# Attention, feed-forward and top-1 experts on one core: low-row folds one block later, the flags in three pieces, the second expert's first weights asked for ahead of its token rows

## The chip, the cores and the metric

The kernel runs on 1 core of one Trainium2 chip, as one launch. The metric is the device time of the launch in microseconds. Three timed runs of the kernel before took 589.20, 590.11 and 590.27 us; their median is 590.11 us. The engines are PE (matrix multiply), DVE (vector), ACT (scalar), POOL and SP; here SP only issues transfers, and POOL does some vector work and the indexed transfers.

## The reference

Three layers are chained. The last one, in which the change lies, is a top-1 mixture of experts over 1536 tokens of width 512, with 8 experts and a hidden width of 1024:

```python
q, k, v  # 2 batches, 8 heads, 768 tokens, head width 64
x = local_and_global_attention(q, k, v)      # 1536 x 512
x = (h * sigmoid(h)) @ w_out,  h = x @ w_in  # hidden width 2048
e_idx = argmax(x @ w_gate)                   # one expert for each token
for e in range(8):
    mask = e_idx == e
    h = np.maximum(x[mask] @ w1[e], 0.0)     # 512 -> 1024
    ye = h @ w2[e]                           # 1024 -> 512
    out[mask] = gate_w[mask, None] * eom[mask, e, None] * ye
```

Operands of matrix multiplies are split into a high and a low part (a rounded copy and the rest), and a product is the sum of high by high, high by low and low by high.

## The kernel before, in words

**Order of the experts.** `order` counts the tokens of each expert and sorts the experts by size. Place 0 is the largest; the places have windows of 320, 272, 248, 224, 208, 192, 184 and 176 rows. In what follows an expert is named by its place p, 0 to 7, so "the second expert" is place 1 and the last is place 7. The token rows, with their factor and their target row, stand sorted by expert in a DRAM buffer `xe`, written there by indexed transfers on POOL.

**One expert.** An expert is 8 blocks of 128 hidden columns, written (p,f) with f from 0 to 7. In the loop of `moe2`, `f1_mm` does the first multiply of a block into a PSUM bank `h` (L678 and L679 when the window is narrow, L684 otherwise); `f1_ev` takes it out: ACT copies the second half (`hs`, L690), DVE adds it (L691), ACT applies the relu and rounds (`hh` or, in the last expert, `hl`, L693), DVE makes the low part (L696). Two blocks later `f2_mm` uses the result in the second multiply into the banks `y` (L706 to L713). The PSUM banks of `h`, of the row turns `xm` and of the fold `yf` are taken in turn from the same four.

**Weights.** The 4 MB of an expert come as 16 units of 128x512, named 0 to 15. `load_u` asks for a unit on SP's queue into one of 8 buffers `qr` (L543); `split_u` has ACT make the high part (L548) and DVE, or POOL for every fourth unit, the low part (L549), which frees the buffer. The units of expert p+1 are split in the blocks f=2 to 7 of expert p (3, 3, 3, 3, 2 and 2 units). The units of an expert are asked for while the expert before it runs: 4 in block f=0, up to 8 in block f=1, and then as buffers come free.

**Rows.** `load_x(p)` asks on SP's queue for the token rows of an expert in tiles of 128 (L653; 3 tiles for the second expert), `load_t(0)` for factors and targets of the first expert (L657). Both read `xe`, so they wait for the last indexed transfer into it. `prep_x` turns the tiles with PE (`xm`, L668) in the blocks f=4 to 6, and ACT and DVE write high and low parts (`xwT`, L670, L671).

**The fold of the low rows.** For five places (0, 1, 5, 6, 7) the last 64 rows share one multiply: high rows give the lower half of a bank, low rows the upper half. `f2_ev` takes them out at the end of an expert: ACT writes `yl` (L721) and `y` (L723), and a function `fold` is put into the list `late`: PE moves the upper half down (`yf`, L727), DVE adds it (L728), POOL scatters the result to `out` (L635). `folds()` runs the list right behind the first multiply of a block. The list is filled in block f=1 of the next expert, so the fold is run in its block f=2; that of the last expert is run in the tail.

**Flags.** `flags` is 14 small DVE instructions (L508 to L521) that compute whether counts fit the windows; the result is read after the last expert (L1133), to decide on a slower general path. It is called in block (7,1), ahead of `f1_ev`.

Each engine takes its instructions in the order of the program, so an instruction that waits holds back all behind it on that engine.

Of the kernel before, what the change touches and what calls it, by code (L numbers as in the profile page):

```python
# [17 lines left out]
ALU = mybir.AluOpType  # L18
AX = mybir.AxisListType
# [4 lines left out]
def kernel(ctx, tc, qk, v, n_global, n_local, w_in, w_out, wg, w1, w2, out):  # L24
# [23 lines left out]
    NE,FF=w1.shape[0],w1.shape[2]  # L48
# [22 lines left out]
    flag=const.tile([P,10],I32,name="flag"); limk=const.tile([P,8],F32,name="limk"); pi=const.tile([P,4],I32,name="pi"); pf=const.tile([P,4],F32,name="pf")  # L71
    ordi=const.tile([P,8],I32,name="ordi"); first=const.tile([P,1],F32,name="first"); firstb=const.tile([P,1],F32,name="firstb"); cntf=const.tile([P,32],F32,name="cntf"); capk=const.tile([P,8],F32,name="capk")
    V=nc.vector; A=nc.scalar; G=nc.gpsimd; T=nc.tensor; S=nc.sync
# [411 lines left out]
    def order(c):  # L485
# [16 lines left out]
        if c==0:  # L502
            V.tensor_copy(first,i)
            V.tensor_scalar(out=first,in0=first,scalar1=-1.0,scalar2=8.0,op0=ALU.mult,op1=ALU.add)
    def flags():

        w=cntf[:,16:32]
        V.tensor_tensor(out=w[:,0:8],in0=w[:,0:8],in1=capk,op=ALU.subtract)  # L508
        V.tensor_scalar(out=s_flag[:,2:10],in0=w[:,0:8],scalar1=0.0,scalar2=None,op0=ALU.is_gt)
        V.tensor_tensor(out=w[:,0:8],in0=w[:,0:8],in1=limk,op=ALU.subtract)  # L510
        V.tensor_scalar(out=w[:,8:9],in0=pf[:,0:1],scalar1=-32.0,scalar2=None,op0=ALU.add)
        V.tensor_scalar(out=w[:,9:10],in0=pf[:,0:1],scalar1=-1.0,scalar2=None,op0=ALU.mult)
        V.tensor_scalar(out=w[:,10:11],in0=pf[:,2:3],scalar1=-97.0,scalar2=None,op0=ALU.add)
        V.tensor_scalar(out=w[:,11:12],in0=pf[:,2:3],scalar1=-1.0,scalar2=1.0,op0=ALU.mult,op1=ALU.add)
        V.tensor_tensor(out=w[:,12:16],in0=pf,in1=pf,op=ALU.mult)
        V.memset(w[:,12:13],0.0)
        V.memset(w[:,14:15],0.0)
        V.tensor_reduce(out=s_flag[:,1:2],in_=w,axis=AX.X,op=ALU.max)
        V.tensor_scalar(out=s_flag[:,1:2],in0=s_flag[:,1:2],scalar1=0.0,scalar2=None,op0=ALU.is_gt)
        V.tensor_reduce(out=s_flag[:,0:1],in_=s_flag[:,1:10],axis=AX.X,op=ALU.max)  # L520
        V.tensor_copy(flag,s_flag)  # L521
    s_flag=const.tile([P,10],F32,name="s_flag")


# [4 lines left out]
    def moe2_open2():  # L529
        es_m.close()  # L530
        m2['b']=es_2.enter_context(tc.tile_pool(name="m2b",bufs=1,side="left"))
    def ereg(p):
        if p not in reg: reg[p]=nc.values_load(ordi[0:1,p:p+1],engines=[mybir.EngineType.SP],min_val=0,max_val=NE-1)
        return reg[p]
    def wtile(name):
        return wp.tile([P,2,512],F32R,tag="wi",name=name,bufs=NWI)
    def load_u(k,i):

        p,q=divmod(k,4); hf=q//2; e=ereg(p)
        r=m2['a'].tile([P,512],F32,tag="qr",name="qr",bufs=NQR); uqr[k,i]=r  # L540
        if q%2==0: src=w1[ds(e,1),i*P:(i+1)*P,hf*512:(hf+1)*512].rearrange("o p f -> p (o f)")
        else: src=w2[ds(e,1),hf*512+i*P:hf*512+(i+1)*P,:].rearrange("o p d -> p (o d)")
        S.dma_start(r,src)  # L543
# [40 lines left out]
    def late_split():  # L584
        xr=xrp[NTT//2-1]
        for t in range(2): ea['l',t]=halves(xr[:,t,:512],(G,V)[t])
# [21 lines left out]
    def early1(hf,part):  # L608
        if part==0: ea['t']=s1bank([P,512],"eh")
        t=ea['t']; x=ea['xT']  # L610
        for k in range(6*part,6*part+6):
            ww,xx=((0,0),(0,1),(1,0))[k//4]; kc=k%4
            T.matmul(t,x[:,xx,kc,:],uq[2*hf,kc][:,ww],start=(k==0),stop=(k==11))
        if part==0: return
        h=m2['a'].tile([P,512],F32,tag="eh",name="ehs",bufs=2); ea['h',hf]=h
        A.activation(out=h,in_=t,func=AF.Relu)
# [13 lines left out]
    def early4():  # L630
        y=m2['a'].tile([P,512],F32,tag="eh",name="eyo",bufs=2)
        A.activation(out=y,in_=ea['y'],func=AF.Copy,scale=ea['x'][:,512:513])
        put(y,ea['x'][:,TOK:TOK+1].bitcast(I32),P)
# [4 lines left out]
    def tiles(p):  # L638

        a,z=R0[p],WIN[p]-(HALF if p in SMALL else 0)  # L640
        t=[(s,min(P,z-s)) for s in range(a,z,P)]+([(z,HALF)] if p in SMALL else [])
        return [(k,s,n) for k,(s,n) in enumerate(t)]
    def folded(p,k): return p in SMALL and k==len(tiles(p))-1
    xwt={}; xwT={}; ixt={}; sct={}
    def paired(p): return WIN[p]-R0[p]<PAIR
    def small(p):
        ixt[p]=m2['b'].tile([P,3],I32,tag="ix",name="ixt",bufs=4)
        sct[p]=m2['b'].tile([P,3],F32,tag="sc",name="sc",bufs=4)
    def load_x(p):
# [35 lines left out]
    def f1_ev(p,f,between=lambda: None):  # L685

        W=WIN[p]-R0[p]; t=h1.pop((p,f)); hh[p,f]=g=wtile("hl").rearrange("p a b -> p (a b)") if p==NE-1 else m2['b'].tile([P,2*WIN[1]],F32R,tag="hh",name="hh",bufs=HB)
        if paired(p):
            u=m2['b'].tile([P,WIN[1]],F32,tag="hs",name="hs",bufs=2)
            A.activation(out=u[:,:W],in_=t[:,W:2*W],func=AF.Copy)  # L690
            V.tensor_tensor(out=t[:,:W],in0=t[:,:W],in1=u[:,:W],op=ALU.add)  # L691
            between()
        A.activation(out=g[:,:W],in_=t[:,:W],func=AF.Relu)  # L693
        z=W-HALF if p in SMALL else W
        for a,b,o in ((0,z,2*W-z),(z,W,W)):
            if a<b: V.scalar_tensor_tensor(out=g[:,o:o+b-a],in0=t[:,a:b],scalar=0.0,in1=g[:,a:b],op0=ALU.max,op1=ALU.subtract)  # L696
        if not paired(p): between()
# [33 lines left out]
    def folds():  # L731
        while late: late.pop(0)()
    nq=[0,0]; NQR=8; NQB=4
# [11 lines left out]
    def moe2():  # L745
        late_split()
        early1(0,0)
        run_gates(2)
        early1(0,1)
        logits(NTT-2)  # L750
        early1(1,0)
        run_gates(1)
        late1()
        run_gates(1)
        early1(1,1)
        run_gates(1)
        early2(0)
        late3()
        order(1)
        moe2_open2()  # L760
        load_x(1); load_t(0)
        early3(0,0)
        early2(1)
        early3(0,1); early3(1,0)
        early3(1,1)
        early4()
        atags[0]=['s1','s1b','a','pv']
        LG=2
        steps=[(p,f) for p in range(NE) for f in range(8)]
        for g in range(len(steps)+LG):  # L770
            if g<len(steps):
                p,f=steps[g]
                def spl():
                    split_u(4*(p+1)+nq[1]//4,nq[1]%4,nq[1]%4==1); nq[1]+=1
                f1_mm(p,f)
                folds()
                if p+1<NE and f==0: nq[:]=[0,0]
                if g==len(steps)-7: flags()
                ns=(0,0,3,3,3,3,2,2)[f] if p+1<NE else 0
                f1_ev(p,f,spl if ns else lambda: None)  # L780
                if p+1<NE:
                    for _ in range(ns-1): spl()
                    while nq[0]<min(16,nq[1]+4*(f+1),nq[1]+NQR): load_u(4*(p+1)+nq[0]//4,nq[0]%4); nq[0]+=1
                    if p and f==0: load_x(p+1)
                    if p==0 and f==5:
                        for k,s,n in tiles(0): tail(0,k,xwt[0][:,k,0:1],xwt[0][:,k,1:2])
                    t=tiles(p+1)
                    px=PX
                    if px<=f<px+len(t): prep_x(p+1,t[f-px][0])
            if g>=LG:  # L790
                p2,f2=steps[g-LG]
                if p2<NE-1:
                    f2_mm(p2,f2)
                    if f2==7: f2_ev(p2)
                    continue
                big,last=tiles(p2)
                if f2==7: f2_mm(p2,0,[big])
                f2_mm(p2,f2,[last])
                if f2==7:
                    f2_ev(p2,[last])  # L800
                    for k in range(1,8):
                        f2_mm(p2,k,[big])
                        if k==2: folds()
                    f2_ev(p2,[big])
# [233 lines left out]
    with tc.manual_schedule():  # L1038
# [22 lines left out]
        steps=[(c,f) for c in range(len(CH)) for f in range(FB)]  # L1061
# [4 lines left out]
        def run_gates(k):  # L1066
            for _ in range(min(k,len(gq))): gq.pop(0)()
        for g in range(len(steps)+LAG):
            live=g<len(steps)
            if live:  # L1070
                c,f=steps[g]
# [110 lines left out]
```

## Time and profile before

| what | value |
|---|---|
| median of three timed runs | 590.11 us (589.20 to 590.27) |
| the profiled execution's own time | 588.92 us |
| its span, first to last instruction | 587.2 us |
| PE busy | 565.8 us (96%), 3939 matrix multiplies |
| DVE, ACT, POOL busy | 389.9, 302.9, 173.3 us |
| mean granted clock of PE | 0.992 of full speed |
| DMA | 106.74 MB, 182 GB/s over the span |

The busy shares are means over the whole span. The experts take its last third: the first multiply of the first expert starts at 395.12 us, the last at 569.41 us. Matrix multiplies overlap in the pipeline, so a busy PE is not a PE at its peak; what counts here is where PE sat idle and what ended the idle time. A row of a timeline gives the start and the length in us, the engine, the line, what is written and read, the count, and in brackets the idle time of that engine before it with what ended it.

### The profile page before, as it was taken

How to read it: one execution, taken by the hardware profiler on the slowest of the kernel's cores; microseconds unless marked ns; L12 is line 12 of the kernel's file. 1: busy time of each engine (PE TensorE's matmuls, PEld its weight loads, DVE VectorE, ACT ScalarE, POOL GpSimd, SP SyncE). 2: the span in 40 equal slices, each digit the busy share in tenths (PEclk: the TensorE clock that was granted, in tenths of full speed). 3: DMA queues.
4: the chain of work that ended last, by engine and by line, in shares of the span. 5: the costliest groups of instructions: out<-in, count | busy, mean ns of one | idle time of the engine just before them, and what ended most of it. 6: DMA issues, size and time to landing. Idle time of an engine off the chain costs nothing.

```text
span 587.2 us, 11814 instructions
## 1 busy us (share of the span) xinstructions
PE 565.8 (96%) x3939; PEld 475.4 (81%) x3939; DVE 389.9 (66%) x1088; ACT 302.9 (52%) x809; POOL 173.3 (30%) x214
## 2 busy tenths in 40 slices
PE   8999999999999999999999999999999999999983
PEld 3567888888888888888899999887787888887862
DVE  6885799998365756674645247646664887987940
ACT  7796334343444446343622326626656667767631
POOL 2367344443132431223111010213231332433311
PEclk9999999999999999999999999999999999999988
DMA  6666467697447877774473349219674668658400
GB/s 215 228 209 198 183 183 232 219 300 257 162 122 161 198 151 163 147 194 129 109 164 125 90 122 354 102 48 333 218 225 144 207 206 282 230 201 284 133 20 22
DMA packets 87530, 106.74 MB, mean 182 GB/s; under 512 B 35980, under 2 KB 50316, under 8 KB 87460
## 3 DMA queue, kind: packets, MB, share of 16 engines
q1 hardware_dynamic: 84692, 98.98, 56.8%
q0 software_dynamic: 2192, 6.39, 3.1%
q8 instruction: 33, 0.54, 0.4%
q10 hardware_dynamic: 576, 0.52, 0.3%
q14 instruction: 37, 0.30, 0.2%
HBM read 87.14 MB, written 17.66 MB: 178 GB/s over the span
## 4 chain that ended last, share of the span: by engine, by line
PE 64%; issue 10%; DVE 9%; ACT 6%; DMA 6%; POOL 3%; SPq 1%; POOLq 0%; DVEq 0%; ACTq 0%
PE s L339 19%; PE s L359 6%; PE s L360 6%; PE s L361 6%; PE qkp L170 3%; PE h L678 3%; DMA qr<-in_w_dram 3%; PE y L711 2%; PE y L713 2%; PE y L712 2%; PE pv L245 2%; PE h L684 2%; PE tp L206 2%; ACT uq L548 2%; PE h L679 2%
## 5 line engine op out<-in xcount | busy, mean ns | idle before, releaser
L339 PEld LDWEIGHTS s<-xT,wi 128*128 128x128 f32 x1152 | 147.4, 190 | 12.0 <-DVE g L348 5.6
L339 PE MATMUL s<-xT,wi 128*128 128x256 f32 x1152 | 152.0, 284 | 1.3 <-DVE xn L233 0.9
L343 ACT ACTIVATE u<-s 128x256 f32<-128x256 f32 x96 | 35.5, 381 | 102.6 <-PE s L339 100.8
L344 DVE SCALAR_TENSOR_TENSOR s<-u,s 128x256 f32<-128x256 f32 x96 | 39.7, 426 | 72.4 <-ACT u L343 72.4
L549 DVE TENSOR_TENSOR uq<-qr,uq 128x512 fp32r<-128x512 f32 x87 | 76.8, 902 | 8.0 <-ACT uq L548 5.8
L359 PE MATMUL s<-woh,g 128*128 128x512 f32 x192 | 79.4, 413 | 0.0
L360 PE MATMUL s<-woh,g 128*128 128x512 f32 x192 | 75.6, 394 | 0.0
L548 ACT ACTIVATE uq<-qr 128x512 fp32r<-128x512 f32 x112 | 66.7, 626 | 4.8 <-DMA qr<-in_w_dram 4.8
L348 DVE TENSOR_TENSOR g<-s,g 128x256 fp32r<-128x256 f32 x96 | 39.3, 422 | 30.9 <-ACT g L347 28.4
L347 ACT ACTIVATE g<-s 128x256 fp32r<-128x256 f32 x96 | 35.6, 381 | 40.8 <-DVE s L344 40.6
L549 POOL TENSOR_TENSOR uq<-qr,uq 128x512 fp32r<-128x512 f32 x25 | 32.3, 1300 | 55.2 <-ACT uq L548 43.9
L190 ACT ACTIVATE t<-t,mx 128x256 f32<-128x256 f32 (+1 forms) x96 | 45.7, 479 | 0.5 <-DVE mx L179 0.5
L359 PEld LDWEIGHTS s<-woh,g 128*128 128x128 f32 x192 | 36.3, 189 | 8.0 <-ACT u L343 2.7
L360 PEld LDWEIGHTS s<-woh,g 128*128 128x128 f32 x192 | 36.3, 189 | 5.2 <-DVE g L348 0.2
L693 ACT ACTIVATE hh<-h 128x192 fp32r<-128x192 f32 (+5 forms) x56 | 19.7, 352 | 39.7 <-DVE h L691 29.1
L361 PE MATMUL s<-wolr,g 128*128 128x512 f32 x128 | 39.7, 391 | 0.0
L635 POOL DMA_INDIRECT out_dram<-y,ixt x17 | 17.7, 1043 | 73.9 <-ACT y L723 33.8
L711 PE MATMUL y<-uq,hh 128*128 128x512 f32 (+1 forms) x88 | 36.7, 417 | 0.0
L197 POOL TENSOR_TENSOR hl<-t,hl 128x512 f16<-128x512 f32 (+1 forms) x18 | 19.9, 1104 | 50.1 <-ACT xT L269 12.2
L712 PE MATMUL y<-uq,hh 128*128 128x512 f32 (+1 forms) x88 | 34.6, 393 | 0.0
L713 PE MATMUL y<-uq,hh 128*128 128x512 f32 (+1 forms) x88 | 34.6, 393 | 0.0
L678 PE MATMUL h<-xwT,uq 128*128 128x448 f32 (+5 forms) x144 | 33.3, 354 | 0.6 <-DVE hh L696 0.4
(269 smaller groups left out, 1074.3 us busy)
## 6 DMA issues: line engine op xcount, KB each, us to landing
qr<-in_w_dram SPq DMA_DIRECT2D x128, 256.0 KB, 4.7
wolr<-wlo_d SPq DMA_DIRECT2D x64, 256.0 KB, 3.7
wiraw<-in_w_in_dram SPq DMA_DIRECT2D x16, 512.0 KB, 5.9
wraw<-in_w_out_dram SPq DMA_DIRECT2D x13, 512.0 KB, 11.2
ring<-in_qk_dram SPq DMA_DIRECT2D x22, 256.0 KB, 6.0
xe<-xe SPq DMA_DIRECT2D x7, 792.0 KB
wlo_d<-wol SPq DMA_DIRECT2D x16, 256.0 KB, 2.2
xw<-xe SPq DMA_DIRECT2D x15, 264.0 KB, 5.0
```

What stands on the lines that cost most here:

```text
L190: A.activation(out=t[:,j,:ce],in_=t[:,j,:ce],func=AF.Exp,scale=-1.0 if 4*n<SB else 0.125,bias=mx[n][:,h:h+1],accum_out=ss[n][:,h:h+1])
L339: T.matmul(t,w[:,ww,kc,:],x[:,xx,kc,:],start=(k==0),stop=(k==11)); k+=1
L344: V.scalar_tensor_tensor(out=t,in0=u,scalar=1.0,in1=t,op0=ALU.add,op1=ALU.mult)
L359: T.matmul(o,g[u][:,0,sl],wh,start=(f==0),stop=False)
L360: T.matmul(o,g[u][:,1,sl],wh,start=False,stop=False)
L361: else: T.matmul(o,g[u][:,0,sl],wl,start=False,stop=(f==FB-1))
L548: A.activation(out=t[:,0],in_=r,func=AF.Copy)
L549: (G if (i%2 if pool is None else pool) else V).tensor_tensor(out=t[:,1],in0=r,in1=t[:,0],op=ALU.subtract)
L678: for kc in range(KC): T.matmul(t[:,:2*W],uq[4*p+2*(f//4),kc][:,0,s],xwT[p,kc][:,:,:W],start=(kc==0),stop=False)
L711: T.matmul(o,hi,w[:,0],start=(f==0),stop=False)
L712: T.matmul(o,g[:,z:z+n],w[:,0],start=False,stop=False)
L713: T.matmul(o,hi,w[:,1],start=False,stop=(f==7))
```

## The change

`folds()` is skipped in block f=2 of every expert, so a fold runs in block f=3. `flags` gets a part number; part 0 runs behind `f1_ev` of block (7,2), part 1 behind that of (7,3), part 2 behind that of (7,4). And all 8 buffers are filled with the first units of the second expert before `load_x(1)` and `load_t(0)` are issued; block (0,0) then starts its count of asked units at 8 (`NQR`).

```diff
-    def flags():
+    def flags(part):
         w=cntf[:,16:32]
+        if part==1:
+            V.tensor_scalar(out=w[:,9:10],in0=pf[:,0:1],scalar1=-1.0,...)
...
+            V.memset(w[:,14:15],0.0)
+            return
+        if part==2:
+            V.tensor_reduce(out=s_flag[:,1:2],in_=w,axis=AX.X,op=ALU.max)
...
+            V.tensor_copy(flag,s_flag)
+            return
         V.tensor_tensor(out=w[:,0:8],in0=w[:,0:8],in1=capk,op=ALU.subtract)
...
         moe2_open2()
+        for k in range(NQR): load_u(4+k//4,k%4)
         load_x(1); load_t(0)
         early3(0,0)
...
                 f1_mm(p,f)
-                folds()
-                if p+1<NE and f==0: nq[:]=[0,0]
-                if g==len(steps)-7: flags()
+                if f!=2: folds()
+                if p+1<NE and f==0: nq[:]=[0 if p else NQR,0]
                 ns=(0,0,3,3,3,3,2,2)[f] if p+1<NE else 0
                 f1_ev(p,f,spl if ns else lambda: None)
+                if p+1==NE and 2<=f<5: flags(f-2)
```

In the listings of the changed kernel below the lines are 4 or 5 higher than in the kernel before (L547 for L543, L657 for L653, L731 for L727 and so on).

SP's queue, from the load of the sorted order on (`ordi`), in the kernel before; `xw` are the rows of the second expert, `xtail` the factors of the first, `qr` the weight units:

```order
L533 TENSOR_LOAD ordi_91
L653 DMA xw_5295<-xe_72 128x528
L653 DMA xw_5297<-xe_72 128x528
L653 DMA xw_5299<-xe_72 128x528
L657 DMA xtail_5303<-xe_72 128x2x16
L543 DMA qr_5359<-in_w1_dram 128x512
L543 DMA qr_5361<-in_w1_dram 128x512
```

The same place of SP's queue in the changed kernel:

```order
L537 TENSOR_LOAD ordi_91
L547 DMA qr_5293<-in_w1_dram 128x512
L547 DMA qr_5295<-in_w1_dram 128x512
L547 DMA qr_5297<-in_w1_dram 128x512
L547 DMA qr_5299<-in_w1_dram 128x512
L547 DMA qr_5301<-in_w2_dram 128x512
L547 DMA qr_5303<-in_w2_dram 128x512
L547 DMA qr_5305<-in_w2_dram 128x512
L547 DMA qr_5307<-in_w2_dram 128x512
L657 DMA xw_5311<-xe_72 128x528
L657 DMA xw_5313<-xe_72 128x528
L657 DMA xw_5315<-xe_72 128x528
```

Eight weight units now stand ahead of the three row tiles and of `xtail`, which comes next; the count of transfers is the same.

PE in the last expert, from the first multiply of block (7,2), in the kernel before:

```order
L678 MATMUL h_7503<-xwT,uq 128x352 x4
L679 MATMUL h_7503<-xwT,uq 128x176 x4
L727 MATMUL yf<-yl,eI 64x512
L706 MATMUL y<-uq,hl 128x512
L707 MATMUL y<-uq,hl 64x512
L678 MATMUL h_7529<-xwT,uq 128x352 x4
L679 MATMUL h_7529<-xwT,uq 128x176 x4
```

The same place of PE in the changed kernel:

```order
L682 MATMUL h_7489<-xwT,uq 128x352 x4
L683 MATMUL h_7489<-xwT,uq 128x176 x4
L710 MATMUL y<-uq,hl 128x512
L711 MATMUL y<-uq,hl 64x512
L682 MATMUL h_7513<-xwT,uq 128x352 x4
L683 MATMUL h_7513<-xwT,uq 128x176 x4
L731 MATMUL yf<-yl,eI 64x512
```

Ten multiplies, the second multiply of block (7,0) and the first of (7,3), moved ahead of the fold of expert 6; the folds of experts 0, 1 and 5 are moved in the same way.

DVE in the last expert, from the end of the flags to block (7,2), in the kernel before (`h_7459` belongs to block (7,1), `h_7503` to (7,2)):

```order
L518 TENSOR_REDUCE s_flag<-cntf 128x1
L519 TENSOR_SCALAR s_flag<-s_flag 128x1
L520 TENSOR_REDUCE s_flag<-s_flag 128x9
L521 CAST flag<-s_flag 128x10
L691 TENSOR_TENSOR h_7459<-h_7459,hs 128x176
L696 SCALAR_TENSOR_TENSOR hl<-h_7459,hl 128x112
L696 SCALAR_TENSOR_TENSOR hl<-h_7459,hl 128x64
L728 SCALAR_TENSOR_TENSOR y<-yf,sc,y 64x512
L691 TENSOR_TENSOR h_7503<-h_7503,hs 128x176
```

DVE in the changed kernel, from block (7,2) (`h_7489`) to the first flag of part 1 (`h_7513` belongs to block (7,3)):

```order
L695 TENSOR_TENSOR h_7489<-h_7489,hs 128x176
L700 SCALAR_TENSOR_TENSOR hl<-h_7489,hl 128x112
L700 SCALAR_TENSOR_TENSOR hl<-h_7489,hl 128x64
L522 TENSOR_TENSOR cntf<-cntf,capk 128x8
L523 TENSOR_SCALAR s_flag<-cntf 128x8
L524 TENSOR_TENSOR cntf<-cntf,limk 128x8
L525 TENSOR_SCALAR cntf<-pf 128x1
L732 SCALAR_TENSOR_TENSOR y<-yf,sc,y 64x512
L695 TENSOR_TENSOR h_7513<-h_7513,hs 128x176
L700 SCALAR_TENSOR_TENSOR hl<-h_7513,hl 128x112
L700 SCALAR_TENSOR_TENSOR hl<-h_7513,hl 128x64
L509 TENSOR_SCALAR cntf<-pf 128x1
```

The flags no longer stand ahead of block (7,1); four of them stand behind (7,2), ahead of the fold.

## Rows read from the trace of the kernel before

**Rows 1.** Waits of PE, 375 to 587.2 us: total, times, longest (us).

```profile
PE yf L727 <- ACT yl L721: 3.9, 2, 2.9
PE h L678 <- DVE hh L696: 1.2, 2, 0.8
PE h L684 <- ACT xwT L670: 0.7, 1, 0.7
PE xm L668 <- DVE xwT L671: 0.4, 1, 0.4
PE xm L668 <- PE h L679: 0.2, 1, 0.2
PE h L678 <- DVE xwT L671: 0.2, 1, 0.2
```

**Rows 2.** Waits of SP's queue, 380 to 430 us: total, times, longest (us).

```profile
SPq L653 <- DMA xe<-xr,gdi: 1.5, 1, 1.5
```

**Rows 3.** Timeline of SP's queue, 384 to 398 us.

```profile
394.52 1.46 SPq L653 DMA_DIRECT2D xw<-xe  x3
...
396.77 1.39 SPq L543 DMA_DIRECT2D qr<-in_w_dram  x3
```

**Rows 4.** Timeline of ACT in expert 0.

```profile
400.95 0.63 ACT L548 ACTIVATE uq<-qr 128x512 fp32r<-128x512 f32 x1 [1.68 <-DMA qr<-in_w_dram]
...
407.38 1.14 ACT L548 ACTIVATE uq<-qr 128x512 fp32r<-128x512 f32 x2
```

**Rows 5.** Timeline of PE in expert 0 and at the start of expert 1.

```profile
403.17 0.60 PE L668 MATMUL xm<-ident,xw 128*128 128x128 f32 x4
...
415.41 1.78 PE L684 MATMUL h<-xwT,uq 128*128 128x272 f32 x12 [0.69 <-ACT xwT L670]
```

**Rows 6.** One stretch of 2 us: busy us by engine, then granted clock, DMA share, GB/s.

```profile
399.00:401.00 2.00, 2.00 (x13) 1.77 (x12) 0.70 (x3) 0.32 (x3) 0.00 (x0) 1.00 0.90 326
```

**Rows 7.** Timeline of PE in experts 6 and 7.

```profile
538.27 0.44 PE L727 MATMUL yf<-yl,eI 64*64 64x512 f32 x1 [1.08 <-ACT yl L721]
...
557.23 0.58 PE L679 MATMUL h<-xwT,uq 128*128 128x176 f32 x4
560.66 0.44 PE L727 MATMUL yf<-yl,eI 64*64 64x512 f32 x1 [2.86 <-ACT yl L721]
...
564.73 0.81 PE L678 MATMUL h<-xwT,uq 128*128 128x352 f32 x4
...
566.29 0.81 PE L678 MATMUL h<-xwT,uq 128*128 128x352 f32 x4
...
572.13 0.40 PE L707 MATMUL y<-uq,hl 128*64 128x512 f32 x1
```

**Rows 8.** One stretch in expert 7, columns as in rows 6.

```profile
561.20:564.70 3.50, 3.50 (x12) 2.99 (x13) 1.58 (x5) 0.95 (x4) 0.42 (x2) 0.51 0.27 73
```

**Rows 9.** Timeline of ACT in expert 7.

```profile
559.10 0.32 ACT L693 ACTIVATE hl<-h 128x176 fp32r<-128x176 f32 x1 [2.24 <-DVE h L691]
...
561.22 0.30 ACT L690 ACTIVATE hs<-h 128x176 f32<-128x176 f32 x1
```

**Rows 10.** Timeline of DVE in experts 6 and 7.

```profile
543.26 2.73 DVE L549 TENSOR_TENSOR uq<-qr,uq 128x512 fp32r<-128x512 f32 x1
...
557.00 0.16 DVE L508 TENSOR_TENSOR cntf<-cntf,capk 128x8 f32<-128x8 f32 x1
...
558.72 0.34 DVE L691 TENSOR_TENSOR h<-h,hs 128x176 f32<-128x176 f32 x1
...
561.36 0.74 DVE L728 SCALAR_TENSOR_TENSOR y<-yf,sc,y 64x512 f32<-64x512 f32 x1 [1.50 <-ACT y L723]
...
569.53 0.35 DVE L691 TENSOR_TENSOR h<-h,hs 128x176 f32<-128x176 f32 x1 [0.36 <-ACT hs L690]
570.26 0.41 DVE L696 SCALAR_TENSOR_TENSOR hl<-h,hl 128x112 fp32r<-128x112 f32 x2 [0.39 <-ACT hl L693]
```

**Rows 11.** Timeline of POOL in expert 6.

```profile
542.89 2.54 POOL L549 TENSOR_TENSOR uq<-qr,uq 128x512 fp32r<-128x512 f32 x2
```

More of the change, by code (lines that the diff above doesn't have):

```diff
@@ L504, in order @@
             V.tensor_scalar(out=first,in0=first,scalar1=-1.0,scalar2=8.0,op0=ALU.mult,op1=ALU.add)
-    def flags():
+    def flags(part):
         w=cntf[:,16:32]
+        if part==1:
+            V.tensor_scalar(out=w[:,9:10],in0=pf[:,0:1],scalar1=-1.0,scalar2=None,op0=ALU.mult)
+            V.tensor_scalar(out=w[:,10:11],in0=pf[:,2:3],scalar1=-97.0,scalar2=None,op0=ALU.add)
+            V.tensor_scalar(out=w[:,11:12],in0=pf[:,2:3],scalar1=-1.0,scalar2=1.0,op0=ALU.mult,op1=ALU.add)
+            V.tensor_tensor(out=w[:,12:16],in0=pf,in1=pf,op=ALU.mult)
+            V.memset(w[:,12:13],0.0)
+            V.memset(w[:,14:15],0.0)
+            return
+        if part==2:
+            V.tensor_reduce(out=s_flag[:,1:2],in_=w,axis=AX.X,op=ALU.max)
+            V.tensor_scalar(out=s_flag[:,1:2],in0=s_flag[:,1:2],scalar1=0.0,scalar2=None,op0=ALU.is_gt)
+            V.tensor_reduce(out=s_flag[:,0:1],in_=s_flag[:,1:10],axis=AX.X,op=ALU.max)
+            V.tensor_copy(flag,s_flag)
+            return
         V.tensor_tensor(out=w[:,0:8],in0=w[:,0:8],in1=capk,op=ALU.subtract)
@@ L511, in flags @@
         V.tensor_scalar(out=w[:,8:9],in0=pf[:,0:1],scalar1=-32.0,scalar2=None,op0=ALU.add)
[L512 to L521, printed above, removed]
     s_flag=const.tile([P,10],F32,name="s_flag")
```

## The prediction

> **What bounds the kernel now.** The page's busy shares name PE (96%), but a share says nothing of single stages, so the second view is the list of PE's waits over the experts [rows 1]: the reader is to see that PE waits in few places, and for ACT or DVE each time. By far the longest is on the fold, 3.9 us in two waits. The third view is the timeline around each wait. In expert 0 there are four (0.8, 0.7, 0.4 and 0.2 us, 2.1 together), the last ahead of expert 1's first multiply [rows 5]; ACT began splitting expert 1's weights only after idling 1.68 us for the first unit [rows 4], and SP had asked for that unit behind the row tiles, which waited 1.5 us for the indexed transfer [rows 2, 3]. In expert 6 the fold holds PE for 1.08 us, in expert 7 for 2.86 us [rows 7]; behind the second wait stands a stretch of 3.5 us at a granted clock of 0.51, the 1.2 GHz level [rows 8]. Elsewhere in the experts PE waits 0.6 us (0.4 of the 1.2 us on `hh`, in expert 5, and 0.2 in expert 2). So the experts are bound by PE, and what a change can win is these waits and the slow stretch: 2.1 + 0.2 + 1.1 + 2.9 us, and the clock.
>
> **Part 1: eight units ahead of the rows.** It removes and adds no instruction; it moves 8 transfers ahead of 4 on SP's queue. The units do not depend on the indexed transfer, so the first goes out when SP began its wait, at 394.52 - 1.5 = 393.0 us, where it went out at 396.77 [rows 2, 3], 3.8 us earlier. It was in ACT's hands 4.2 us after its issue (400.95) [rows 3, 4], with three row tiles of 264 KB ahead of it; so it lands by 397.2, ACT's idle 1.68 us goes, and the splitting on ACT and DVE runs 1.68 us earlier. The first three of PE's waits (0.8, 0.4, 0.2) are smaller than that and go. PE then comes to expert 1 at 415.41 - 2.1 = 413.3; the rows it needs there are ready 1.68 us before 415.41, at 413.7. A wait of 0.4 stays, and the gain is 1.7 us; ACT's second, shorter waits for units go as well, so I take 1.8, with 2.1 as the most.
>
> What is late next? First the rows. The three units issued from 396.77 took 1.39 us, the last 0.33 of it its own, so a step is 0.53 us [rows 3]; eight are 4.2 us, and the tiles go out at 397.3, 2.8 us later than before. PE turns the first at 403.17 [rows 5]. Ahead of it lie 8 x 262 KB = 2.1 MB, and it has 0.27 MB itself: 7.3 us at the 326 GB/s of 399 to 401 us [rows 6]. The first unit's 4.2 us held 2.5 us of row tiles at that rate, so the bare delay is 1.7 us: the tile lands at 393.0 + 1.7 + 7.3 = 402.0, 1.2 us in time. If the whole 4.2 us were delay it would land at 404.5, and PE would wait 1.3 us: then 0.5 of the gain is left. Second, unit 8, which needs the buffer of unit 0. That is free some 1.4 us after ACT takes unit 0 at 399.3; 4.2 us later, at 404.9, unit 8 is there. ACT took it in the second half of the pair at 407.38 [rows 4], so about 407.9, and now wants it at 406.2: 1.3 us in time. The bounds of this part are -0.5 us (both cushions wrong by 2 us) and 2.1 us.
>
> The Trainium skill ("DMA: Bandwidth & Descriptors", section on queues, rings and completion order) says that each DMA engine consumes the descriptors of SP's queue in ring order. That speaks against this part, since the tiles cannot pass the 2.1 MB; no row here shows the order inside a ring. An estimate by that page's fit (2.0 us and the bytes at 436 GB/s) puts the first tile at 400.4, in time as well; the measured rate above decides.
>
> **Part 2: the fold in block f=3.** Five folds exist; four move, none changes in size. In experts 1 and 2 PE did not wait on the fold [rows 1], and the moved one is covered by the same PE work: nothing. In expert 6 the wait of 1.08 us goes, because the second multiply of (6,0) and the first of (6,3), now stand ahead of the fold; in the narrower expert 7 such a pair takes 1.56 us [rows 7]. DVE must follow: right there one of its splits took 2.73 us [rows 10] beside two splits run back to back on POOL [rows 11]. The scatter of the fold now stands between those two on POOL, so this stall should shorten, and DVE gains more than PE does. I take 1.0, between 0 (DVE is as late as before and PE waits for it at the end of the expert) and 1.1. The 0.2 in expert 2 is of the same kind, a split on DVE held up by POOL behind scatters; I take all of it, 0.2.
>
> The Trainium skill ("SBUF — State Buffer", section on who interferes with whom) says that a DVE instruction with two SBUF inputs and a POOL instruction that reads SBUF block each other for a whole instruction. The rows agree so far as 2.73 us stands beside POOL's 2.54; by that rule one POOL split alone would hold DVE for some 1.3 us, an estimate by which DVE wins 1.4 us.
>
> **Part 3: flags and fold in the last expert.** The flags hold DVE from 557.00 to 558.72, 1.72 us for 14 instructions [rows 10]. Behind them stands the DVE part of (7,1), for which ACT waits 2.24 us; behind that on ACT come the copies that the fold needs [rows 9], and PE waits 2.86 us [rows 7]. Without the flags there all of this comes 1.72 us earlier: the fold could start at 560.66 - 1.72 = 558.9. PE ends the first multiply of (7,2) at about 557.23 + 0.42 = 557.65; one block of first and second multiply takes 1.56 us (566.29 - 564.73) [rows 7], which now stands ahead of the fold, so PE comes to it at 559.2: no wait. Nor should the clock fall, since 1.08 us of waiting in expert 6 left it at full speed. At 0.51 for 3.5 us the work of 1.8 us was done, so the slow stretch cost 1.7 us [rows 8]. The most that this part can give is 2.86 + 1.7 = 4.6 us.
>
> What is late next is DVE. ACT's `hs` of (7,2) starts at 561.22 - 1.72 = 559.5 [rows 9], so DVE starts (7,2) at 559.85. A block takes it 1.14 us from 569.53 to the end of the low part [rows 10]; six blocks are 6.84, the flags, all of which still lie in this stretch, 1.72, the fold 0.74: 9.3 us, to 569.15. The second multiply of (7,7), which needs this, ended its pair with the row at 572.13 [rows 7]; so the gain by DVE's chain is 2.9 us, and by the overlap of instructions on DVE a few tenths more. If DVE enters the expert earlier, as part 2 makes likely, the chain starts earlier and the gain nears 4.6. I take 3.6. The lower bound is 1.7: only the flags' own time is won, and short waits for `hl` keep the rest.
>
> **Sum.** 1.8 + 0.2 + 1.0 + 3.6 = 6.6 us against the profiled execution's 588.92: 582.3. That execution was 1.2 us below the median of the runs, so as a median 583.5.
>
> **Rivals.** (a) Expert 0 gives it back: rows or unit 8 land 2 us later than worked out and PE waits there instead. For it: SP's queue is one line, and 2.1 MB were put ahead; against it: two cushions of 1.2 and 1.3 us. Part 1 is then 0, the sum 4.8, the time 585.3. (b) DVE becomes the bound of experts 6 and 7: the fold's wait turns into waits for `hh` and `hl`. For it: the 9.3 us chain above; against it: the 1.72 us ahead of (7,1) do leave. 1.8 + 0.2 + 0 + 1.7 = 3.7 us, 586.4. (c) The change does not do what it says: the fold waits in f=3 as it did in f=2, since `yl` comes late for another reason, or DVE's stalls beside POOL move to a worse place. Within 1.2 us of 590.1. (d) Slower, by one mechanism: PE waits at 403.17 for the first row tile so long that its clock falls too. A wait of 2.86 us cost 1.7 us of clock [rows 7, 8]; parts 2 and 3 still give 4.8, so it decides from a wait of 4.3 us on (4.8 + 1.2 - 1.7). The tile would land at 407.5, 2.4 MB in 12.8 us, 185 GB/s against 326 [rows 6]. A wait of 5.5 us would make 592.5.
>
> **How the numbers follow.** Forecast 0.64, (a) 0.14, (b) 0.13, (c) 0.05, (d) 0.04. 0.2% of the time, 1.2 us, is about what a measurement of this kernel tells from no change. (a) and (b) are faster by more than that: faster 0.91, same 0.05, slower 0.04. The forecast's own range is 581.8 to 585.3. With all upper bounds (2.1, 0.2, 1.1, 4.6: 8.0 us) the median is 582.1, and the runs scatter by 1.1 us: 581.0. Upwards the range takes in (a) and (b) with 0.9 us of scatter: 587.3.
>
> **What would show it.** Right: SP issues `qr` at about 393 and `xw` at about 397.3; ACT does not wait for the first unit; no wait of PE above 0.5 us in expert 0; no PE wait on `yf` in experts 6 and 7; the clock at 1.00 through expert 7; there, short waits of PE on `hl`, up to 0.6 us each. Wrong: PE waiting at `xm` of expert 0 or ACT waiting for unit 8 (part 1); a PE wait on `yf` in f=3 (parts 2 and 3); DVE's low part of (7,7) ending later than about 10 us behind the first multiply of (7,2).

## The result and the profile after

The changed kernel takes 583.33 us (median of four runs, 582.61 to 585.12) against 589.72 for the kernel before in its four (589.2 to 590.27): ratio 0.9896, 95% interval 0.9871 to 0.9921. That is 0.2 us from the forecast of 583.5 and inside both ranges. The profiled execution took 582.61 us with a span of 580.8, 6.4 us less span than before.

To see where the 6.4 us come from, the timeline of PE is cut at the first multiply of each expert (`h` by L678 before, L682 after); expert 7 is counted to the start of the last `y` multiply. The start of expert 0 shifts by up to 1.6 us from run to run for reasons ahead of the change, so these lengths are a cleaner measure than the spans.

| us | e0 | e1 | e2 | e3 | e4 | e5 | e6 | e7 |
|---|---|---|---|---|---|---|---|---|
| before | 20.29 | 27.00 | 24.81 | 22.22 | 21.57 | 20.33 | 20.74 | 25.74 |
| after | 18.06 | 26.98 | 24.35 | 22.11 | 21.60 | 20.28 | 20.39 | 22.57 |
| gain | 2.23 | 0.02 | 0.46 | 0.11 | -0.03 | 0.05 | 0.35 | 3.17 |
| forecast | 1.8 | 0 | 0.2 | 0 | 0 | 0 | 1.0 | 3.6 |

The waits of PE in the experts after the change (total, times, longest), which answer to [rows 1]:

```profile
PE h L682 <- DVE hh L700: 0.8, 2, 0.5
PE y L710 <- DVE hl L700: 0.7, 2, 0.4
PE xm L672 <- DMA xw<-xe: 0.4, 1, 0.4
```

Both waits on `yf` are gone, 3.9 us; what is left is 1.9 us, and two of its three kinds were not there before.

SP's queue, to be held against [rows 3]:

```profile
392.75 4.36 SPq L547 DMA_DIRECT2D qr<-in_w_dram  x8
397.85 1.83 SPq L657 DMA_DIRECT2D xw<-xe  x3
```

ACT's first split of expert 1's weights, which stood behind 1.68 us of idling [rows 4], and now behind none:

```profile
399.18 0.63 ACT L552 ACTIVATE uq<-qr 128x512 fp32r<-128x512 f32 x1
```

PE in expert 0, at the start of expert 1 and in experts 6 and 7, against [rows 5, 7]:

```profile
403.76 0.63 PE L672 MATMUL xm<-ident,xw 128*128 128x128 f32 x4 [0.40 <-DMA xw<-xe]
...
413.21 1.77 PE L688 MATMUL h<-xwT,uq 128*128 128x272 f32 x12
...
536.62 0.44 PE L731 MATMUL yf<-yl,eI 64*64 64x512 f32 x1
...
541.59 0.91 PE L682 MATMUL h<-xwT,uq 128*128 128x368 f32 x4 [0.48 <-DVE hh L700]
...
556.22 0.45 PE L731 MATMUL yf<-yl,eI 64*64 64x512 f32 x1
...
560.31 0.47 PE L710 MATMUL y<-uq,hl 128*128 128x512 f32 x1 [0.36 <-DVE hl L700]
...
564.56 0.48 PE L710 MATMUL y<-uq,hl 128*128 128x512 f32 x1 [0.34 <-DVE hl L700]
```

The reader is to see three things: a new wait of 0.40 for the first row tile; the fold (`yf`) without a wait in both experts; and in the place of each fold's wait, 4 to 8 us later, shorter ones on what DVE writes.

Granted clock in the stretch that was at 0.51 [rows 8] (busy us by engine, then clock, DMA share, GB/s), and, as the last row, the stretch up to PE's first row tile, which answers to [rows 6]:

```profile
555.00:560.00 5.00, 4.94 (x30) 4.11 (x29) 2.40 (x12) 2.69 (x8) 1.53 (x2) 1.00 0.19 49
560.00:565.00 5.00, 4.35 (x24) 3.52 (x25) 3.30 (x22) 1.88 (x7) 0.43 (x1) 1.00 0.03 7
...
393.00:403.60 10.60, 10.36 (x61) 9.23 (x59) 5.14 (x14) 5.48 (x14) 2.26 (x2) 1.00 0.97 309
```

PE stays at its upper level, 2.4 GHz, throughout expert 7. What the DMA queues moved within the last of these stretches (packets, MB, share of the 16 engines; q1 is SP's, q0 that of POOL's indexed transfers), first from 393.0 to 393.6 us, then from 393.7 to 402.8:

```profile
q0 software_dynamic: 58, 0.24, 103.9%
...
q1 hardware_dynamic: 1299, 2.39, 89.0%
q0 software_dynamic: 92, 0.26, 7.2%
```

So SP's units, asked for from 392.75 on, move from 393.7 on; what moved before them was an indexed transfer.

DVE in experts 6 and 7, against [rows 10]:

```profile
538.24 1.37 DVE L553 TENSOR_TENSOR uq<-qr,uq 128x512 fp32r<-128x512 f32 x1 [0.25 <-ACT uq L552]
539.53 0.73 DVE L732 SCALAR_TENSOR_TENSOR y<-yf,sc,y 64x512 f32<-64x512 f32 x1
...
557.84 0.16 DVE L522 TENSOR_TENSOR cntf<-cntf,capk 128x8 f32<-128x8 f32 x1
...
558.38 0.73 DVE L732 SCALAR_TENSOR_TENSOR y<-yf,sc,y 64x512 f32<-64x512 f32 x1
...
565.05 0.41 DVE L700 SCALAR_TENSOR_TENSOR hl<-h,hl 128x112 fp32r<-128x112 f32 x2 [0.39 <-ACT hl L697]
568.31 0.74 DVE L732 SCALAR_TENSOR_TENSOR y<-yf,sc,y 64x512 f32<-64x512 f32 x1 [2.86 <-ACT y L727]
```

POOL in expert 6, against [rows 11]:

```profile
537.77 1.28 POOL L553 TENSOR_TENSOR uq<-qr,uq 128x512 fp32r<-128x512 f32 x1 [1.62 <-ACT uq L552]
540.54 1.37 POOL L639 DMA_INDIRECT out_dram<-y,ixt  x1 [1.49 <-DVE h L695]
542.01 1.29 POOL L553 TENSOR_TENSOR uq<-qr,uq 128x512 fp32r<-128x512 f32 x1
```

The scatter now parts POOL's two splits, and DVE's long split is 1.37 us where it was 2.73. In expert 7 DVE still has all 14 flag instructions between the low part of (7,2) and that of (7,5), though it stands idle for 2.86 us at the end of the expert.

### The profile page after: what moved, and what is told of

Same layout as the page of the kernel before. It is cut to its first block, busy times and chain, and to the rows that moved or that the text cites. A ratio compares the mean times of both kernels' runs of the same rounds, so it can differ in the third digit from the quotient of the medians.

```text
span 580.8 us, 11817 instructions
## 1 busy us (share of the span) xinstructions
PE 564.0 (97%) x3939; PEld 474.1 (82%) x3939; DVE 387.0 (67%) x1088; ACT 302.2 (52%) x809; POOL 173.8 (30%) x214
## 4 chain that ended last, share of the span: by engine, by line
PE 71%; DVE 11%; issue 6%; ACT 5%; POOL 3%; DMA 3%; SPq 1%; POOLq 0%; DVEq 0%; ACTq 0%
PE s L339 17%; PE s L359 6%; PE s L360 5%; PE s L361 5%; PE h L682 5%; PE qkp L170 3%; PE y L715 3%; PE y L717 3%; PE y L716 3%; PE h L683 3%; POOL wol L323 2%; PE pv L245 2%; DVE wt L296 2%; PE h L688 2%; PE tp L206 2%
## 5 line engine op out<-in xcount | busy, mean ns | idle before, releaser
L553 DVE TENSOR_TENSOR uq<-qr,uq 128x512 fp32r<-128x512 f32 x87 | 70.6, 832 | 4.9 <-ACT uq L552 2.7
L697 ACT ACTIVATE hh<-h 128x192 fp32r<-128x192 f32 (+5 forms) x56 | 19.7, 353 | 38.3 <-DVE h L695 27.7
L695 DVE TENSOR_TENSOR h<-h,hs 128x192 f32<-128x192 f32 (+5 forms) x56 | 20.8, 371 | 21.6 <-ACT hs L694 13.7
```

The lines of the kernel that those rows point to most:

```text
L553: (G if (i%2 if pool is None else pool) else V).tensor_tensor(out=t[:,1],in0=r,in1=t[:,0],op=ALU.subtract)
```

## The experiments

Eleven kernels ran, in three groups; each group is compared with runs of the kernel before made beside it (medians 590.13, 589.84 and 590.16 us). Ratios are to that, with 95% intervals; lengths are those of the table above.

| kernel | median us | ratio | interval | e0 | e2 | e5 | e6 | e7 |
|---|---|---|---|---|---|---|---|---|
| units ahead only | 587.67 | 0.9960 | 0.9945 to 0.9975 | 18.30 | 24.66 | 19.73 | 20.62 | 25.64 |
| fold in f=3 only | 586.40 | 0.9940 | 0.9923 to 0.9958 | 20.69 | 24.35 | 20.28 | 20.39 | 23.10 |
| flags in pieces only | 586.12 | 0.9937 | 0.9913 to 0.9961 | 20.40 | 24.56 | 20.28 | 20.85 | 22.36 |
| units and flags, fold back in f=2 | 584.20 | 0.9904 | 0.9879 to 0.9930 | 18.52 | 24.78 | 19.72 | 20.64 | 22.33 |
| after + fold's bank | 583.07 | 0.9871 | 0.9844 to 0.9897 | 18.05 | 24.35 | 20.28 | 20.41 | 22.53 |
| after + flags at the end | 582.86 | 0.9868 | 0.9841 to 0.9895 | 18.69 | 24.35 | 20.05 | 20.38 | 21.36 |
| after + four units ahead | 583.67 | 0.9883 | 0.9853 to 0.9913 | 19.41 | 24.35 | 20.28 | 20.40 | 22.56 |
| all three of these | 583.69 | 0.9888 | 0.9863 to 0.9913 | 19.05 | 24.35 | 20.28 | 20.42 | 21.35 |
| after, again | 582.69 | 0.9884 | 0.9866 to 0.9902 | 18.05 | 24.35 | 19.72 | 20.18 | 22.57 |
| flags at the end, first tile behind six | 581.98 | 0.9866 | 0.9846 to 0.9886 | 18.05 | 24.34 | 20.28 | 20.39 | 21.37 |
| after + two units split by POOL | 582.72 | 0.9881 | 0.9861 to 0.9901 | 18.06 | 24.35 | 19.72 | 20.17 | 22.34 |

### Each part alone

**Units ahead only** (the kernel before, with):

```diff
+        for k in range(NQR): load_u(4+k//4,k%4)
         load_x(1); load_t(0)
...
-                if p+1<NE and f==0: nq[:]=[0,0]
+                if p+1<NE and f==0: nq[:]=[0 if p else NQR,0]
```

> The kernel before with the eight weight units ahead of the row tiles and nothing else. Theory (each part gives what its stage gained in the trace after): expert 1's first multiply comes 2.2 us earlier than in the kernel before, with one wait of PE of about 0.4 us for the first row tile, and nothing of it is given back later: 2.2 us faster, ratio 0.9963. Rival (the gain hangs on the other parts: the experts after it are paced by ACT and DVE and give it back): 0 to 1 us faster, ratio above 0.998, and the lead of 2.2 us shrinks from expert 1 to expert 7.

Expert 0 went from 20.29 to 18.30 us, 2.0 (the three kernels without this part took 20.29, 20.40 and 20.69), and nothing else moved by more than 0.15 but expert 5, which varies by itself (last section). The waits of PE:

```profile
PE yf L727 <- ACT yl L721: 3.8, 2, 2.8
PE xm L668 <- DMA xw<-xe: 0.7, 1, 0.7
```

and the clock of the two stretches around the second wait on the fold, in the same kernel:

```profile
555.00:560.00 5.00, 2.20 (x8) 1.30 (x7) 2.77 (x17) 2.37 (x5) 1.03 (x1) 0.82 0.13 25
560.00:565.00 5.00, 5.00 (x30) 4.70 (x29) 1.92 (x8) 1.59 (x5) 0.93 (x1) 0.84 0.08 29
```

Part 1 acts by itself and does nothing for expert 7: the wait of 2.8 us and the slow stretch are both still there.

**Fold in f=3 only:**

```diff
-                folds()
+                if f!=2: folds()
```

> The kernel before with the folds in block f=3 and nothing else; all 14 flags stay ahead of block (7,1). Theory (the last expert is paced by DVE's chain once the 2.86 us wait and the slow clock are gone, and the flags cost DVE the same 1.7 us wherever they stand in it): PE's wait on the fold in expert 7 falls from 2.86 to about 1.4 us, the clock stays at 1.00, the last expert gains about 2.9 us; with 0.8 us in experts 2 and 6: 3.7 us faster, ratio 0.9937. Rival (the parts add up, and flags and fold each hold half of the last expert's 3.2 us): 0.8 + 1.6 = 2.4 us, ratio 0.9959, with a clock that still falls.

Expert 7 became 2.64 us shorter, expert 6 0.35 and expert 2 0.46; of the fold's waits one is left, and expert 7's clock stays up:

```profile
PE yf L727 <- ACT yl L721: 1.3, 1, 1.3
...
555.00:560.00 5.00, 5.00 (x32) 4.49 (x31) 4.33 (x22) 1.33 (x5) 0.49 (x1) 1.00 0.00 0
560.00:565.00 5.00, 3.63 (x20) 2.81 (x20) 2.09 (x8) 3.27 (x9) 1.03 (x1) 1.00 0.20 52
```

**Flags in pieces only:**

```diff
-                if g==len(steps)-7: flags()
...
+                if p+1==NE and 2<=f<5: flags(f-2)
```

> The kernel before with the flags in three pieces and nothing else; the folds stay in f=2. Theory (DVE's chain paces the last expert, and either edit alone takes the slow clock away): PE's wait on the fold in expert 7 falls from 2.86 to 1.1 us, the one in expert 6 stays at 1.1, the clock stays at 1.00; the last expert gains about 3 us: ratio 0.9949. Rival (the parts add up, half of the 3.2 us each): 1.6 us, ratio 0.9973.

Expert 7 became 3.38 us shorter, more than in the changed kernel. The fold's waits in experts 6 and 7 are 1.1 and 1.0 us, and the clock of all of expert 7 is 1.00:

```profile
PE yf L731 <- ACT yl L725: 2.2, 2, 1.1
...
555.00:560.00 5.00, 3.98 (x23) 3.19 (x22) 2.73 (x11) 2.99 (x9) 1.03 (x1) 1.00 0.00 0
560.00:565.00 5.00, 5.00 (x33) 4.51 (x32) 3.63 (x22) 2.05 (x7) 0.93 (x1) 1.00 0.20 51
```

**Units and flags, the folds back in f=2:**

```diff
-                if f!=2: folds()
+                folds()
```

> The changed kernel with the folds back in block f=2. Theory (either edit alone gives most of the last expert's gain): 2.2 us from the units and about 3 us in the last expert, 0.8 us in experts 2 and 6 missing: 5.2 us faster than before, ratio 0.9912, about 1.1 us slower than the changed kernel. Rival (the parts add up): 2.2 + 1.6 = 3.8 us, ratio 0.9936.

By time it can't be told from the changed kernel. By stage, the moved fold is worth 0.43 us in expert 2 and 0.25 in expert 6 (0.46 against the second profile of the changed kernel, 20.18, in which expert 5 was as short as here), and costs 0.24 in expert 7, where PE waits 1.02 us for the fold and then for nothing.

These four answer the main question. The two edits of expert 7 are not two gains: each alone shortens the wait of 2.86 us to 1.3 or 1.0, and with that each takes away the whole slow stretch. Alone they gain 2.64 and 3.38 us there, together 3.17. So the three single ratios multiply to 0.984, and the whole change measures 0.9896.

### What paces what is left

**The fold's bank.** In the changed kernel the fold takes its PSUM bank in f=3, and the bank's next user was suspected in the new wait of 0.48 us in expert 6. Here the bank is taken in the turn of f=2, as before the change:

```diff
-                m=abank([P,512],"yf")
+                m=held.pop() if held else abank([P,512],"yf")
...
                 if f!=2: folds()
+                elif late: held.append(abank([P,512],"yf"))
```

> The changed kernel, with the fold's PSUM bank taken in the turn of block f=2 as in the kernel before, while the fold itself runs in f=3. Theory (the moved fold shifted the turn of the four banks, so that the first multiply of (6,5) needs the bank of (6,3), which DVE clears late behind the fold): PE's wait of 0.5 us on `hh` in expert 6 goes, expert 6 takes 19.9 instead of 20.4 us, 0.5 us faster than the changed kernel, ratio to before 0.9888. Rival (DVE paces expert 6 and the bank is only where PE notices): the wait shows up elsewhere, expert 6 takes 20.3 to 20.4 us, the time is that of the changed kernel.

Expert 6 is 20.41 us, as after the change. PE's wait has only moved one block on, to (6,6):

```profile
545.28 0.92 PE L682 MATMUL h<-xwT,uq 128*128 128x368 f32 x4 [0.52 <-DVE hh L700]
```

The bank decides where PE notices that DVE is late, not how late it is.

**All flags behind the last block:**

```diff
-                if p+1==NE and 2<=f<5: flags(f-2)
+                if p+1==NE and f==7:
+                    for part in range(3): flags(part)
```

> The changed kernel, with all 14 flags behind the last `f1_ev`, block (7,7), where DVE sat idle for 2.9 us. Theory (DVE's chain with the flags in it paces the last expert): DVE's low part of (7,7) is done about 1.7 us earlier, PE's two waits on `hl` go, the last expert takes 21.2 to 21.6 instead of 22.6 us: 1.0 to 1.4 us faster than the changed kernel, ratio 0.9876. Rival (ACT's copies out of the banks pace the start of the chain, the flags lie in DVE's gaps): 0 to 0.3 us.

Expert 7 is 21.36 us, 1.2 less than after the change, and PE waits for no `hl`. The end of DVE's work in this kernel:

```profile
564.75 0.41 DVE L700 SCALAR_TENSOR_TENSOR hl<-h,hl 128x112 fp32r<-128x112 f32 x2 [0.38 <-ACT hl L697]
565.07 0.16 DVE L522 TENSOR_TENSOR cntf<-cntf,capk 128x8 f32<-128x8 f32 x1
...
566.70 0.17 DVE L520 CAST flag<-s_flag 128x10 int32<-128x10 f32 x1
567.57 0.74 DVE L732 SCALAR_TENSOR_TENSOR y<-yf,sc,y 64x512 f32<-64x512 f32 x1 [0.70 <-PE yf L731]
```

The 14 instructions fit into DVE's idle time with 0.7 us to spare. So in the changed kernel it was the flags in DVE's chain, as the prediction's own chain had them, that kept expert 7 from its best.

**Four units ahead instead of eight:**

```diff
-        for k in range(NQR): load_u(4+k//4,k%4)
+        for k in range(4): load_u(4+k//4,k%4)
...
-                if p+1<NE and f==0: nq[:]=[0 if p else NQR,0]
+                if p+1<NE and f==0: nq[:]=[0 if p else 4,0]
```

> The changed kernel, with four units ahead of the row tiles instead of eight. Theory (the tiles wait behind the bytes ahead of them on one queue): the row tiles go out 2.1 us earlier, PE's wait of 0.4 us for the first tile goes, and expert 0 takes 17.6 to 17.7 instead of 18.1 us: 0.4 us faster than the changed kernel. Rival (units 4 to 7, now behind the rows, are late for ACT): ACT waits 0.5 to 1.5 us for unit 4, and expert 0 takes 18 to 18.6 us.

The row tile is in time, but expert 0 takes 19.41 us, 1.35 more, above what either forecast allowed. ACT waits for a unit:

```profile
407.61 1.29 ACT L552 ACTIVATE uq<-qr 128x512 fp32r<-128x512 f32 x2 [1.28 <-DMA qr<-in_w_dram]
```

and PE for what ACT and DVE then deliver late, at a row tile and at expert 1's first multiply:

```profile
410.27 0.66 PE L672 MATMUL xm<-ident,xw 128*128 128x128 f32 x4 [0.95 <-DVE xwT L675]
...
415.07 1.14 PE L688 MATMUL h<-xwT,uq 128*128 128x272 f32 x7 [0.68 <-ACT xwT L674]
```

**All three of these edits together:**

> The changed kernel with the three edits together: the fold's bank taken in f=2, all flags behind (7,7), four units ahead. Theory: 0.5 + 1.2 + 0.4 = 2.1 us faster than the changed kernel, ratio to before 0.986. Rival (each gain is given back by DVE's pace in the experts between): 0.5 to 1 us, ratio 0.988 or more.

Nothing new: expert 7 keeps what the flags gain (21.35), expert 0 what the four units lose (19.05), and the time is that of the changed kernel.

**The changed kernel again** (no edit), as the measure for the last group:

> The changed kernel once more, beside the kernels of this group on the same chip, with more rounds. Expected by every theory: ratio to before 0.989 to 0.990; PE's wait for the first row tile between 0.4 and 1.1 us (it was that in the runs with eight units ahead); expert 7 takes 22.6 us.

It repeats every stage to 0.04 us except experts 5 and 6, which are 0.56 and 0.21 shorter by chance.

**Flags at the end, and the first row tile behind six units:**

```diff
-        load_x(1); load_t(0)
+        small(1)
         for k in range(NQR):
+            if k==6: load_x(1,tiles(1)[:1])
             load_u(4+k//4,k%4)
+        load_x(1,tiles(1)[1:]); load_t(0)
```

> The changed kernel with two edits: all flags behind (7,7), and the first row tile of the second expert asked for behind six weight units instead of eight, the other two tiles behind all eight. Theory: the tile goes out 1.1 us earlier, PE's wait for it (0.4 to 1.1 us) goes and units 6 and 7, half a microsecond later, are still in time, so expert 0 takes 17.6 to 17.8 us; the last expert takes 21.4: 1.6 to 2.2 us faster than the changed kernel, ratio to before 0.986 to 0.987. Rival (what is saved at the rows is lost at the units, as with four ahead): ACT waits for unit 6 or 7 and expert 0 takes 18.2 us or more; then only the 1.2 us of the flags stay, ratio 0.9875.

All waits of PE in the experts:

```profile
PE h L683 <- DVE hh L701: 0.8, 2, 0.5
PE h L689 <- ACT xwT L675: 0.5, 1, 0.5
```

The wait for the row tile is gone, ACT waits 0.51 us for unit 8, PE 0.50 at expert 1's first multiply, and expert 0 is 18.05 us all the same. That the tile's earlier place made unit 8 late is not shown: with all eight units ahead ACT waited between 0 and 0.71 us for it. With the flags' 1.2 us this is the fastest kernel, 581.98 us. Its interval overlaps that of the changed kernel beside it (0.9866 against 0.9884), so only the stage is settled: expert 7 was 21.35 to 21.37 us in all three kernels with the flags at the end, 22.34 to 22.57 in all others with the changed order.

**Two units of expert 6 split by POOL instead of DVE:**

```diff
-                    split_u(..., nq[1]%4==1); nq[1]+=1
+                    split_u(..., nq[1]%4==1 or (p==6 and nq[1] in (7,11))); nq[1]+=1
```

> The changed kernel with units 7 and 11 of the last expert, which DVE splits during expert 6, given to POOL (six units on POOL there instead of four). Theory (DVE's work paces expert 6, so that most of the fold's 1.08 us was no gain): DVE is relieved of 2 splits of 0.7 us, PE's wait on `hh` of 0.5 us goes, expert 6 takes 19.7 to 20.0 instead of 20.4 us. Rival (POOL and DVE hold each other up when both split at once): DVE's other splits beside POOL's grow from 0.7 to 1.2 us or more, and expert 6 takes 20.3 us or more.

Expert 6 is 20.17 us, 20.18 in the changed kernel of the same group. The wait was in place before the moved units are split:

```profile
540.57 0.91 PE L682 MATMUL h<-xwT,uq 128*128 128x368 f32 x4 [0.37 <-DVE hh L700]
```

So this run could not relieve the wait and doesn't confirm that DVE's splitting sets expert 6. Beside POOL's moved split one of DVE's took 1.46 us, where it took 0.68 in the changed kernel, as the rival said. Expert 7 is 0.23 us shorter than in the changed kernel; no run explains that.

## Why the prediction was right, and where it was not

The total was right by 0.2 us, the sum of gains by 0.2 (6.6 forecast, 6.4 found), and no term was off by more than 0.65. The terms are not all right for the reasons given: experts 0 and 2 gave 0.7 us more than forecast, experts 6 and 7 1.1 us less, so that the total came so near is in part luck.

**Part 1, 1.8 forecast, 2.23 found.** The mechanism held: SP asks for the units at 392.75 (about 393 forecast), ACT no longer waits for the first one, and PE's waits of 0.8, 0.7, 0.4 and 0.2 are gone. The gain is larger because ACT's next wait for a unit went too:

```profile
402.27 1.27 ACT L548 ACTIVATE uq<-qr 128x512 fp32r<-128x512 f32 x2 [0.47 <-DMA qr<-in_w_dram]
```

1.68 and 0.47 us make 2.15; the prediction took 0.1 for the second.

Wrong was the landing of the first row tile: 402.0 forecast, 1.2 us in time; PE could start on it only at 403.76, after a wait of 0.40 us. By the text's own mark ("PE waiting at `xm` of expert 0") the cushion failed. The mis-sized term is the "7.3 us at the 326 GB/s of 399 to 401 us". That rate is of all queues; in the kernel before they moved in these 2 us:

```profile
q1 hardware_dynamic: 313, 0.42, 61.0%
q0 software_dynamic: 70, 0.23, 28.7%
```

That is 210 GB/s for SP's queue alone. After the change SP's queue moved the 2.39 MB of eight units and one tile from 393.7 to 402.8: 9.1 us, 263 GB/s, 1.8 us more than forecast. What lay outside the bytes, 1.0 us from the issue to the first of them and 1.0 from the last to PE's start, is near the 1.7 taken. The bound of 1.3 us, given for the worst reading, held in every run (0 to 1.08 with eight ahead). The Trainium skill ("DMA: Bandwidth & Descriptors", section on queues, rings and completion order) has each engine consume the queue in ring order; the late tile agrees with it, and the trace has the first packets of the row tiles (2112 bytes long, a unit's 2048) at 401.68, when the units are nearly through. The estimate by that page's fit in the prediction, 400.4, was 3.4 us early; here the measurement decides. The other mark, ACT waiting for unit 8, did not show in the changed kernel, but ACT waited 0.11 to 0.71 us for it in four of the other six profiles with eight units ahead: that cushion of 1.3 us was not there either.

Why the wait for the tile cost nothing: with 0, 0.28, 0.40 and 0.46 us of it expert 0 took 18.05 or 18.06 us each time, with 0.70, 0.92 and 1.08 it took 18.30, 18.52 and 18.69. From some 0.45 us on, then, a tenth of wait costs a tenth, and below that nothing. Below it ACT's last write of expert 1's rows sets the end; after the change and, in the second line, before:

```profile
412.78 0.38 ACT L674 ACTIVATE xwT<-xm 128x256 fp32r<-128x256 f32 x1
...
414.98 0.38 ACT L670 ACTIVATE xwT<-xm 128x256 fp32r<-128x256 f32 x1
```

In both kernels expert 1's first multiply follows 0.05 us behind its end, and that end lies 17.98 to 18.02 us behind the start of expert 0 in seven of the eight profiles with six or eight units ahead of the tile, 18.13 in the other. In the two of them where the tile came in time PE waited for this write, 0.15 us (the run with the bank) and 0.50. The 0.4 us of wait that the prediction left for this place PE had already spent at the row tile; that the failed cushion cost nothing is luck. What paces ACT itself there, its own splitting or DVE's, no run tested alone.

**Part 2, 0.2 + 1.0 forecast, 0.46 + 0.35 found.** This is the mis-sized step: "In expert 6 the wait of 1.08 us goes ... DVE must follow ... I take 1.0". The wait went, in f=3 the fold finds its input ready, and DVE's stall beside POOL shrank as said, from 2.73 to 1.37 us. The prediction's estimate by the rule of the Trainium skill ("SBUF — State Buffer", section on who interferes with whom) was some 1.3 us beside a single POOL split, and the trace agrees. But DVE did not follow: at the start of (6,4) PE is 1.12 us ahead of its place in the kernel before, at (6,5), where it waits 0.48 us on `hh`, 0.46, and at the end of the expert 0.35. Between kernels with the same length of expert 5 the move is worth 0.46 in expert 6 (20.85 against 20.39, 20.64 against 20.18). Rival (b) was right for expert 6 by half. The run with the bank shows that the lateness is DVE's. What DVE should give up to catch up stays open: the run with two units on POOL moved work that lies behind the wait. In expert 2 the same move gave 0.46, all of it ahead of expert 3's first multiply (the listed wait of 0.2 there counts from the modelled end of the multiply before): (2,7) starts 21.6 us into the expert in both kernels. Two of DVE's splits there, 4.92 us before, take 2.24 after. With the fold in f=2 the second of them ended 20.72, 20.82, 20.95 and 20.97 us into the expert, and the expert took 24.56, 24.66, 24.78 and 24.81 us; with the fold in f=3 it ended at 20.1 or earlier, and the expert took 24.34 or 24.35 in all nine kernels. There DVE's gain reached PE, in expert 6 most of it did not.

**Part 3, 3.6 forecast, 3.17 found.** The causes were right: the flags ahead of (7,1) led to the wait of 2.86 us, that wait led to the slow stretch, and both go. DVE's chain then decides, as the text said; it gave "2.9 us, and by the overlap of instructions on DVE a few tenths more", and that, 3.17, is what came. The step on top, to 3.6, is the one that failed: "If DVE enters the expert earlier ... the chain starts earlier". DVE took up (7,2) 3.2 us behind the start of PE's first multiply (553.50 to 556.72), 3.3 in the prediction's working. The chain itself was shorter than the 9.3 us forecast, 8.7 to 565.46; but PE's last wait is for the low part of (7,6), at 564.56, and behind it only PE's own work is left, so what DVE gains there is lost on PE. The text's mark for this, an end of the low part of (7,7) later than about 10 us behind PE's first multiply of (7,2), was badly set: it came 10.9 us behind the end of that multiply (554.57), while the chain worked out in the same text already allowed 11.5.

What the prediction did not see is that the flags and the fold are two ways to the same gain. Next to the flags the moved fold is worth -0.24 us in expert 7; without them it is worth 2.64. Flags at the end with the fold in f=2 was not run.

**The other rivals.** Expert 0 gave nothing back (a), though the tile came 1.8 us later than worked out, nearly the 2 us of that rival; its price was too high, since behind the cushion of 1.2 us only 0.8 of the 2 could have become a wait, and 1.0 of part 1's 1.8 was left. And the fold did wait less (c). Of the slower case (d) the wait exists, at a tenth of the 4.3 us from which it would decide.

## What to carry to other kernels

Two edits that shorten the same long wait don't add: price them as alternatives, with the clock that falls behind the wait as part of the one gain. Where a side computation must run on a busy engine, look for that engine's longest idle stretch before cutting it in pieces: here 2.86 us stood free at the end, and whole flags there beat pieces by 1.2 us. When loads are put ahead of others on a queue, check both queues of consumers: eight units ahead cost the rows up to 1.1 us, of which what was above some 0.45 reached the end of the stage; four cost ACT 1.3, and all of it did. And a rate read off a stretch belongs to all queues that moved in it: here a queue alone had two thirds of it.

## What the runs showed of the hardware that was not expected

**The clock.** A wait of PE of 2.8 or 2.9 us in expert 7 was followed by a drop to the 1.2 GHz level (0.51 over 3.5 us [rows 8]); waits of 1.0 to 1.3 us at the same place left it at 1.00 in three kernels. By the prediction's working the drop cost 1.7 us, more than half as much as the wait.

**Expert 5 has several lengths**, 20.3 or 19.7 us, once 20.05, in kernels whose order there is the same, and even for the same kernel. In each a DVE split is held beside two POOL splits that run back to back behind a scatter. The longest DVE split of expert 5 in the changed kernel's first profile:

```profile
518.82 3.67 DVE L553 TENSOR_TENSOR uq<-qr,uq 128x512 fp32r<-128x512 f32 x1
```

POOL there:

```profile
518.18 1.18 POOL L639 DMA_INDIRECT out_dram<-y,ixt  x1 [3.06 <-PE y L711]
519.38 1.31 POOL L553 TENSOR_TENSOR qb<-qr,qb 128x512 fp32r<-128x512 f32 x1
520.63 1.30 POOL L553 TENSOR_TENSOR uq<-qr,uq 128x512 fp32r<-128x512 f32 x1
```

and DVE in its second profile, where the scatter took 0.92 us and expert 5 19.72:

```profile
519.34 2.91 DVE L553 TENSOR_TENSOR uq<-qr,uq 128x512 fp32r<-128x512 f32 x1
```

POOL's pair starts 0.6 us behind DVE's split in the first profile and 0.2 us ahead of it in the second (519.15). How long DVE is held thus goes with where it meets POOL's pair, and 0.6 us of the program hang on that, half of what the flags' place is worth; a single profile can't tell such a gain from chance.
